# Which arm of a guard's branch stands next to it: `preferred_fallthrough_block=False` on a branch that is never taken into its body

## The chip, the cores, the metric

One core of one Trainium2 chip. The metric is the device time of one execution, in microseconds (us). Nine runs of the kernel before on one chip took 1291.71 to 1295.97 us, a spread of 4.3 us or 0.33%, so an effect of 2 us is at the edge of what times alone can show. This document therefore leans on traces, and on one length in them, called the **tail**: from the start of the last weight load on PE (TensorE) to the end of the span. The work ahead of that point is identical in the kernels compared, except where said, and in this tail PE has only 0.27 us of matmuls left to finish.

## The reference, cut to what matters

```python
x = A_x                                            # 2048 x 1024
h = _layernorm(x) * (1 + ca) + sa
x = x + ga * attention(h @ wq, k_cache, v_cache) @ wo   # 32 heads, softmax over 512 keys
h = _layernorm(x) * (1 + cb) + sb
x = x + gb * ((silu(h @ w_gate) * (h @ w_up)) @ w_down)
```

The kernel has a fast path that leaves out the maximum in the softmax. While it runs it bounds the scores. If the bound is over a limit, a flag is set, and a general path computes everything again. For the given inputs the flag is 0, so the general path never runs. It is still in the program: 16,921 instructions on PE, 3,010 on DVE (VectorE), 1,988 on ACT (ScalarE), 493 on SP (SyncE) and 59 on POOL (GpSimd).

## The kernel before

The guard, whole:

```python
def tile_adaLN_cond__sliding_block_cached__swiglu_ffn__prompt_kernel(tc, *args):
    nc = tc.nc
    with tc.tile_pool(name="guard", bufs=1) as gp:
        flag = gp.tile([1, 1], I32, name="flag")
        fast_path(tc, flag, *args)
        over = nc.values_load(flag[0:1, 0:1], min_val=0, max_val=1)   # L1243
        with tc.If(over > 0):                                         # L1244
            general_path(tc, *args)
```

The end of the fast path: the down projection of each tile of rows, whose outputs ACT sends off. The last tile is cut in three pieces.

```python
    def emit_down(cc, dh, t, widths=(512,)):
        ...
        for w in widths:
            ...                                   # 28 matmuls into d_ps          L1188
            nc.vector.tensor_tensor(out=r, in0=d_ps, in1=gb_bc[:, dsl], op=ALU.mult)          # L1192
            nc.vector.tensor_tensor(out=o, in0=r, in1=xt[cc * QT + t][:, dsl], op=ALU.add)    # L1194
            nc.scalar.dma_start(out=out2d[row:row + P, dsl], in_=o)                           # L1195
```

All weights are loaded by SP, whose last issue comes some 26 us before the last weight load on PE.

How the guard is built decides this case. The trace of before shows on each of the five engines one load of the flag (`TENSOR_LOAD`, L1243, 479 to 546 ns) and one compare-and-branch (L1244), at its own time: 686.7 us on POOL, 1258.4 on SP, 1284.3 on PE, 1285.9 on DVE, 1286.5 on ACT. Behind the branch stand three blocks:

- the **true block**, which is the general path;
- the **false block**, a few waits and semaphore updates, still of line 1244: on SP eight waits for all DMAs of the fast path, the last outputs among them; on ACT, DVE and PE one each, for their own last instruction;
- the **end block** of line 1271: on SP twelve closing waits for every engine and every DMA queue, then a barrier of all engines. Each engine has `DRAIN` instructions of this line; its first one (in before at 1288.3 us on PE, 1288.9 on DVE, 1289.2 on ACT and on SP) is read here as its arrival at the barrier.

The waits and updates are of semaphores, with which the program orders its engines and DMAs; the views list them as `EVENT_SEMAPHORE`. In the views a name with q at its end (SPq, ACTq) is an engine's instruction sequencer; PE's stands under PEldq.

Before the change the order is true, false, end. With the flag at 0 every engine jumps over its whole general path.

Of the kernel before, what the change touches and what calls it, by code (L numbers as in the profile page):

```python
# [1237 lines left out]
# [3 lines that stand above are left out]
        flag = gp.tile([1, 1], I32, name="flag")  # L1241
        fast_path(tc, flag, *args)
        over = nc.values_load(flag[0:1, 0:1], min_val=0, max_val=1)  # L1243
        with tc.If(over > 0):  # L1244
            general_path(tc, *args)


# [28 lines left out]
```

## Time and profile before

| | |
|---|---|
| median of 3 runs | 1292.92 us (1292.06 to 1293.39) |
| span of the profiled run | 1290.07 us, granted clock 0.999 |
| PE busy | 1271.4 us, 99% |
| start of the last weight load | 1284.63 us |
| tail | 5.44 us |

From the page of before, the span, the busiest engine, and the chain of waits that ended last:

```profile
span 1290.1 us, 15319 instructions
PE 1271.4 (99%) x6073; PEld 577.4 (45%) x6193; DVE 653.1 (51%) x1159; ACT 433.7 (34%) x625; POOL 1.2 (0%) x7
...
PE 95%; SPq 2%; DMA 1%; DVE 1%; issue 1%; DVEq 0%
```

PE bounds the kernel to its last matmul. The change touches no tile instruction, so only the tail can answer to it. Branches and semaphore instructions are not counted as busy; they show when the trace is asked for one source line. The view of line 1244 of before (count, then shortest/median/longest duration in ns, then the start of the first and of the last):

```profile
L1244 SPq EVENT_SEMAPHORE  x8: 17/17/17, 1265.3 to 1287.8; - x8
L1244 POOLq EVENT_SEMAPHORE  x5: 17/43/43, 687.1 to 687.5; - x5
L1244 POOLq COMPARE_BRANCH  x1: 45/45/45, 686.7 to 686.7; - x1
...
L1244 SPq COMPARE_BRANCH  x1: 58/58/58, 1258.4 to 1258.4; - x1
L1244 PEldq COMPARE_BRANCH  x1: 3762/3762/3762, 1284.3 to 1284.3; - x1
L1244 DVEq COMPARE_BRANCH  x1: 76/76/76, 1285.9 to 1285.9; - x1
L1244 ACTq COMPARE_BRANCH  x1: 65/65/65, 1286.5 to 1286.5; - x1
L1244 PEldq EVENT_SEMAPHORE  x1: 51/51/51, 1288.2 to 1288.2; - x1
L1244 DVEq EVENT_SEMAPHORE  x1: 21/21/21, 1288.8 to 1288.8; - x1
L1244 ACTq EVENT_SEMAPHORE  x1: 17/17/17, 1289.1 to 1289.1; - x1
```

Read each engine's branch against its next instruction. ACT branches at 1286.5 and goes on at 1289.1; DVE at 1285.9 and 1288.8; PE's branch itself lasts 3.8 us. POOL, with 59 instructions to jump over, goes on after 0.4 us. In each of the three gaps lies a DMA packet of one of the two instruction queues (from the trace's packet records, us from the last weight load):

```
before: PE   branch -0.29   packet of 16384 bytes  1.12 to 2.06   goes on at 3.53
        DVE  branch  1.27   packet of  8192 bytes  2.30 to 2.75   goes on at 4.15
        ACT  branch  1.90   packet of  8192 bytes  2.84 to 3.25   goes on at 4.50
```

(The first packet is of queue q8, whose 50 packets make 0.82 MB; the other two are of q14, and so are those put down to SP. Which packet is whose is inferred from the order and the times.) So the silence, 2.6 us on ACT, 2.9 on DVE and 3.8 on PE, is read as a wait for instructions that have to be fetched. Of before alone this is an inference; runs 7 to 9 and 11 test it.

SP is different. It branched at 1258.4, then spent 29 us waiting for output DMAs anyway, so its fetch cost nothing. The packet is there, at 1262.48 to 1262.79; before_again has one at the same place (4.0 and 4.6 us after SP's branch), and the traces in which SP falls through have none in the 25 us after the branch. The view of line 1271 of before, and then SP's waits after 1283 us:

```profile
L1271 SPq EVENT_SEMAPHORE  x14: 17/28/362, 1287.9 to 1290.0; - x14
...
L1271 SPq DRAIN  x3: 7/7/12, 1289.2 to 1289.5; - x3
L1271 PEldq DRAIN  x2: 8/8/8, 1288.3 to 1289.6; - x2
L1271 DVEq DRAIN  x2: 10/14/17, 1288.9 to 1289.5; - x2
L1271 ACTq DRAIN  x2: 8/8/8, 1289.2 to 1289.5; - x2
```

```profile
SPq L1271 <- DVEq L1244: 0.4, 1, 0.4
SPq L1271 <- ACTq L1244: 0.3, 1, 0.3
```

SP passes the last output's semaphore at 1287.8 (last wait of line 1244) and starts its closing waits at once, at 1287.9. Two of them are held by the late DVE and ACT. Its drain comes at 1289.2, and the end 0.86 us after it.

### The profile page before, as it was taken

The page shows a single profiled execution, that of the slowest core. Times are in us where ns is not written, and L with a number is a line of the kernel's source. Part 1 is how long each engine was busy: PE and PEld are TensorE (multiplying, and loading weights), DVE is VectorE, ACT ScalarE, POOL GpSimd, SP SyncE. Part 2 cuts the span into 40 slices and gives each one's busy share as a digit, 9 for nine tenths or more (in the row PEclk, how much of TensorE's full clock was granted, in tenths as well). Part 3 has the DMA queues.
Part 4 walks back from the last instruction along what each step waited for, and adds up shares of the span by engine and source line. Part 5 has one row for each costly group of instructions (what it writes and reads, how often), then busy time and mean ns, then how long its engine had stood idle before and what let it go on. Part 6 is the DMA issues. An engine that isn't in the chain of part 4 may idle for free.

```text
span 1290.1 us, 15319 instructions
## 1 busy us (share of the span) xinstructions
PE 1271.4 (99%) x6073; PEld 577.4 (45%) x6193; DVE 653.1 (51%) x1159; ACT 433.7 (34%) x625; POOL 1.2 (0%) x7
## 2 busy tenths in 40 slices
PE   8999999999999999999999999999999999999998
PEld 4444444444444444444444444444444444444444
DVE  5575668976688867597865641222122111222122
ACT  4755545554555555555552111011100111011100
POOL 0000000000000000000000000000000000000000
PEclk9999999999999999999999999999999999999999
DMA  9788565567365655455657485454536445454402
GB/s 290 242 277 256 178 196 139 170 174 219 103 193 144 189 146 175 146 165 143 185 194 238 127 240 182 136 192 131 171 105 220 157 148 178 135 192 131 147 18 84
DMA packets 219939, 221.08 MB, mean 171 GB/s; under 512 B 45385, under 2 KB 205129, under 8 KB 219858
## 3 DMA queue, kind: packets, MB, share of 16 engines
q1 hardware_dynamic: 214690, 215.54, 54.5%
q10 hardware_dynamic: 5168, 4.46, 1.0%
q8 instruction: 50, 0.82, 0.3%
q14 instruction: 31, 0.25, 0.1%
HBM read 207.63 MB, written 4.47 MB: 164 GB/s over the span
## 4 chain that ended last, share of the span: by engine, by line
PE 95%; SPq 2%; DMA 1%; DVE 1%; issue 1%; DVEq 0%
PE gu_ps L1168 29%; PE a_ps L1095 17%; PE q_ps L1018 17%; PE d_ps L1188 15%; PE o_ps L1079 9%; PE s_ps L1031 8%; SPq L664 1%; PE l_ps L1048 1%; SPq L703 1%; DMA hT<-xn 0%; DMA wq<-in_A_wq_dram 0%; DMA wu<-in_B_w_up_dram 0%; PE row_ps L777 0%; DVE guT L1174 0%; DVE xn L833 0%
## 5 line engine op out<-in xcount | busy, mean ns | idle before, releaser
L1033 ACT ACTIVATE pT<-s_ps 128x1024 bf16<-128x1024 f32 x256 | 252.0, 1026 | 72.8 <-PE s_ps L1031 67.3
L1095 PE MATMUL a_ps<-wo,oT 128*128 128x512 bf16 x972 | 238.9, 379 | 2.6
L1018 PE MATMUL q_ps<-hT,wq 128*128 128x512 bf16 x994 | 236.1, 379 | 0.8 <-DVE modT L753 0.3
L1173 ACT ACTIVATE sg<-gu_ps 128x512 bf16<-128x512 f32 x112 | 66.9, 597 | 486.0 <-PE gu_ps L1168 420.4
L1174 DVE TENSOR_TENSOR guT<-gu_ps,sg 128x512 bf16<-128x512 f32 x112 | 77.4, 691 | 280.0 <-ACT sg L1173 280.0
L1168 PE MATMUL gu_ps<-hT,wu 128*128 128x512 bf16 x878 | 210.1, 379 | 2.6 <-DMA wu<-in_B_w_up_dram 1.7
L1168 PE MATMUL gu_ps<-hT,wg 128*128 128x512 bf16 x877 | 210.0, 379 | 1.1
L1188 PE MATMUL d_ps<-wd,guT 128*128 128x512 bf16 (+2 forms) x934 | 193.2, 366 | 0.9
L1095 PEld LDWEIGHTS <-oT 128*128 128x128 bf16 x1024 | 100.0, 98 | 121.4 <-issue 1.3
L1018 PEld LDWEIGHTS <-wq 128*128 128x128 bf16 x1000 | 97.8, 98 | 118.5 <-DMA wq<-in_A_wq_dram 0.7
L1188 PEld LDWEIGHTS <-guT 128*128 128x128 bf16 x952 | 90.9, 98 | 103.0
L1168 PEld LDWEIGHTS <-wu 128*128 128x128 bf16 x896 | 87.6, 98 | 107.8 <-DMA wu<-in_B_w_up_dram 2.2
L1168 PEld LDWEIGHTS <-wg 128*128 128x128 bf16 x896 | 87.7, 98 | 105.7
L1038 DVE TENSOR_TENSOR psA<-pT 128x1024 bf16<-128x1024 bf16 x128 | 87.8, 686 | 89.0 <-ACT pT L1033 88.9
L1031 PE MATMUL s_ps<-qT,kT 128*128 128x512 bf16 x508 | 131.1, 379 | 0.7 <-ACT pT L1033 0.6
L1079 PE MATMUL o_ps<-pT,v_sb 128*128 128x512 bf16 x510 | 131.5, 380 | 0.2
L1081 ACT CAST oT<-o_ps 128x512 bf16<-128x512 f32 x128 | 74.5, 582 | 166.4 <-PE o_ps L1079 166.4
L914 DVE CAST qT<-q_ps 128x512 bf16<-128x512 f32 x128 | 87.5, 685 | 78.6 <-PE q_ps L1018 77.9
L1031 PEld LDWEIGHTS <-kT 128*128 128x128 bf16 x512 | 50.1, 98 | 61.5 <-issue 1.5
L1069 DVE TENSOR_TENSOR oT<-oT,rb 128x1024 bf16<-128x1024 bf16 x64 | 75.4, 1218 | 1.5 <-DMA rb<-r_d 1.5
L1079 PEld LDWEIGHTS <-v_sb 128*128 128x128 bf16 x512 | 47.4, 98 | 60.3 <-issue 7.7
L1040 DVE TENSOR_TENSOR psB<-psA 128x512 bf16<-128x512 bf16 x128 | 53.4, 417 | 0.6
(279 smaller groups left out, 443.2 us busy)
## 6 DMA issues: line engine op xcount, KB each, us to landing
wq<-in_A_wq_dram SPq DMA_DIRECT2D x64, 512.0 KB
rb<-r_d SPq DMA_DIRECT2D x64, 512.0 KB
wo<-in_A_wo_dram SPq DMA_DIRECT2D x64, 512.0 KB
wg<-in_B_w_gate_dram SPq DMA_DIRECT2D x56, 512.0 KB
wu<-in_B_w_up_dram SPq DMA_DIRECT2D x56, 512.0 KB
wd<-in_B_w_down_dram SPq DMA_DIRECT2D x56, 512.0 KB
wmr<-in_w_mod_dram SPq DMA_DIRECT2D x8, 1024.0 KB
out_dram<-o_sb ACTq DMA_DIRECT2D x31, 128.0 KB
```

The costliest lines, as they stand in the source:

```text
L914: nc.vector.tensor_copy(out=t, in_=q_ps)
L1018: nc.tensor.matmul(q_ps, lhsT=wq_tiles[(cc, h // 4, dt // 4)][:, dt % 4, (h % 4) * P:(h % 4 + 1) * P], rhs=hT[("h1", cc)][:, dt, :], start ...
L1031: nc.tensor.matmul(s_ps[:, i, :], lhsT=kT[:, kv, j * P:(j + 1) * P], rhs=qT[g], start=True, stop=True)
L1033: nc.scalar.activation(out=p[:, 2 * jj:2 * jj + 2, :], in_=s_ps, func=ACT.Exp, scale=scale)
L1038: nc.vector.tensor_tensor(out=a, in0=p[:, 0:2, :], in1=p[:, 2:4, :], op=ALU.add)
L1069: pin(nc.vector.tensor_tensor(out=oo, in0=oo, in1=rb, op=ALU.mult))
L1079: nc.tensor.matmul(o_ps, lhsT=v_sb[:, kv, j, :], rhs=pT[g][:, j, :], start=(j == 0), stop=(j == WT - 1))
L1081: nc.scalar.copy(out=oT[(cc, hg)][:, hi, :], in_=o_ps)
L1095: nc.tensor.matmul(a_ps, lhsT=oT[(cc, 2 * q + i)][:, hh % 4, t * P:(t + 1) * P], rhs=wo_tiles[(cc, q, dh, i)][:, hh % 4, :], start=(hh == ...
L1168: nc.tensor.matmul(ps[:, n, :], lhsT=gu_w[(cc, fg, nm, dt // 4)][:, dt % 4, fi * P:(fi + 1) * P], rhs=hT[("h2", cc)][:, dt, :], start=(dt ...
L1174: nc.vector.tensor_tensor(out=guT[(cc, fg)][:, fi, :], in0=ps[:, 1, :], in1=g, op=ALU.mult)
L1188: nc.tensor.matmul(d_ps, lhsT=guT[(cc, f // 4)][:, f % 4, t * P:(t + 1) * P], rhs=wd_tiles[(cc, dh, f // 4)][:, f % 4, c0:c0 + w], start=( ...
```

## The change

The intent: the usual case should fall through the branch and not jump.

```diff
-        with tc.If(over > 0):
+        with tc.If(over > 0, preferred_fallthrough_block=False):
             general_path(tc, *args)
```

The order of the built instructions tells more than the diff. Here PE's; the other engines are alike:

```
  L1243 TensorLoad flag
  L1244 CompareAndBranch
+ L1244 UnconditionalBranch
  L263  Ldweights ...                 (the general path begins)
  ...
  L578  Matmult ...                   (the general path ends)
- L1244 UnconditionalBranch x2
+ L1244 UnconditionalBranch
```

The order is now false, true, end. The usual case falls through into the false block, and that block ends with an unconditional jump over the general path to the end block.

A sentence is cut from the prediction that follows: it gave a rule for such waits that came from no trace of this case. No term of the sum goes with it: the sum came to +2.0 to +2.3 us, and its 2.6 to 2.9 us for SP are an estimate from the gaps of ACT (2.60) and DVE (2.88) in the trace of before.

> **What bounds the kernel.** The page of before: PE busy 1271.4 of 1290.1 us (99%), full clock; the chain that ended last is 95% PE. The change touches no tile instruction. It can move only the tail after the last matmul (1284.9 us), 5.2 us without PE work.
>
> **The tail now, from the trace's records of lines 1243, 1244 and 1271** (start times, us):
> - The last DVE op ends at 1285.56; ACT issues the last output DMA at 1285.59; it lands at 1287.76.
> - The branch is taken in the usual case, over the general path to the "false" block and end block behind it. After their compare-and-branch the engines go silent: ACT 1286.53 to 1289.12 (2.60 us), DVE 1285.90 to 1288.78 (2.88), PE 1284.34 to 1288.10 (3.76). In each gap lies an instruction-queue packet (8 KB; PE 16 KB) 0.9 to 1.4 us after the branch. POOL, whose general path is short, resumes after 0.42 us with none. [...]
> - SP branched at 1258.45; its fetch was hidden behind its wait for output DMAs. It passes the last output's semaphore at 1287.78, then makes 12 closing waits about 0.062 us apart, two of them held 0.5 us in all by DVE's and ACT's late arrival. Its drain at 1289.21 is followed 0.86 us later by the end.
>
> **What the change does.** By the instruction order, the false block now stands right after the branch, and ends in an unconditional jump over the general path to the end block. The far jump is not removed but moved: from before the false block's waits to after them.
> - ACT, DVE, PE: completion semaphores go out without the fetch (ACT 1286.6 instead of 1289.12); then they fetch, and reach the end barrier at about the old time. SP's 0.5 us of holds go.
> - SP: its false block waits for the last output (1287.76), and only then jumps over 493 instructions. Its fetch, hidden before, is exposed. Estimate from ACT's and DVE's gaps: 2.6 to 2.9 us.
>
> **Sum (estimate).** SP leaves its false block at 1287.86, resumes at 1290.5 to 1290.8, 12 waits 0.75 us, then 0.86 us: end 1292.1 to 1292.4 against 1290.07: +2.0 to +2.3 us, all on the critical path, 0.17%. Predicted 1295.0 us, range 1292.8 to 1296.6, mostly run scatter (1292.06 to 1293.39 before). Slower, though the wording promises a gain; within 2% almost surely.
>
> **What would show each step.**
> - ACT and DVE: line 1244's wait within about 0.1 us of the branch (PE: after its last matmul), then a gap of at least 2.5 us before line 1271.
> - SP: last wait of line 1244 at the output's landing, first of line 1271 2.5 to 3 us later, an 8 KB instruction packet between; then 12 waits 0.062 us apart, none held.
> - Nothing changed before 1284.9 us.
>
> **What would make it wrong.** If the sequencer fetches an unconditional jump's target while SP waits, or holds it already, the stall vanishes: about -0.5 us (1292.4). If SP's end block straddles a fetch boundary, it stalls twice: +4 us; by packet times I read a boundary every 128 instructions, none inside that block. Drift between sessions may hide 2 us.
>
> Chances: faster by over 2% 0.005, within 2% 0.985, slower 0.01.

## The result, and the profile after

| | before | after |
|---|---|---|
| runs | 1292.06 to 1293.42, median 1293.16 (4) | 1294.76 to 1297.00, median 1296.47 (4) |
| ratio, 95% interval | | 1.0025 (1.0011 to 1.0040) |
| span of the profiled run | 1290.07 | 1295.14 |
| start of the last weight load | 1284.63 | 1287.42 |
| tail | 5.44 | 7.72 |

All runs count as fast: the slowest of before is 0.11% above the fastest, the slowest of after 0.17%. A ratio is the mean time of one kernel's fast runs over that of the other's of the same rounds, so it is not quite the ratio of the medians quoted. The change is slower, by about 0.25%, well inside the 2% that count as the same. Of the 5.07 us between the two spans, 2.28 are in the tail, and 2.79 are ahead of it, where nothing was changed.

The page of after, the lines that answer to those above:

```profile
span 1295.1 us, 15444 instructions
PE 1280.3 (99%) x6193; PEld 577.9 (45%) x6193; DVE 653.1 (50%) x1159; ACT 433.7 (33%) x625; POOL 1.2 (0%) x7
...
PE 97%; DMA 1%; DVE 1%; SPq 0%; ACT 0%; issue 0%; DVEq 0%
```

(The 120 more matmuls are records that the first trace lacks, not work.) The tail, in the view of line 1244 of after:

```profile
L1244 SPq EVENT_SEMAPHORE  x8: 17/17/17, 1267.9 to 1290.9; - x8
...
L1244 SPq COMPARE_BRANCH  x2: 38/48/57, 1261.2 to 1291.0; - x2
L1244 PEldq COMPARE_BRANCH  x2: 95/1684/3273, 1287.1 to 1287.9; - x2
L1244 DVEq COMPARE_BRANCH  x2: 51/55/59, 1288.7 to 1288.9; - x2
L1244 ACTq COMPARE_BRANCH  x2: 38/44/51, 1289.3 to 1289.5; - x2
...
L1244 PEldq EVENT_SEMAPHORE  x1: 51/51/51, 1287.7 to 1287.7; - x1
L1244 DVEq EVENT_SEMAPHORE  x1: 21/21/21, 1288.8 to 1288.8; - x1
L1244 ACTq EVENT_SEMAPHORE  x1: 17/17/17, 1289.4 to 1289.4; - x1
```

Each engine now shows two branches: the compare, not taken, and the jump. ACT's and DVE's semaphores follow the compare within 0.1 us; the wait for instructions is gone from that place. It has moved behind the second branch, as the view of line 1271 of after shows:

```profile
L1271 SPq EVENT_SEMAPHORE  x14: 17/28/28, 1293.5 to 1295.1; - x14
...
L1271 SPq DRAIN  x3: 7/7/13, 1294.3 to 1294.6; - x3
L1271 PEldq DRAIN  x2: 8/40/73, 1291.2 to 1294.7; - x2
L1271 DVEq DRAIN  x2: 10/34/57, 1291.8 to 1294.6; - x2
L1271 ACTq DRAIN  x2: 8/44/80, 1292.1 to 1294.6; - x2
```

ACT jumps at 1289.5 and reaches its drain at 1292.1; counted from the last weight load that is 4.67, against 4.58 before. Nothing is won there. SP jumps at 1291.0, right after the last output's semaphore (1290.9), and its first closing wait starts at 1293.5. In the gap of 2.5 us lie four packets of the instruction queues. The first, of 8 KB, from 1291.91 to 1292.39, comes 0.92 us after SP's jump, as DVE's and ACT's came 0.94 to 1.02 us after their branches before; the other three come 0.6 us after DVE and ACT and 1.3 us after PE have gone on. That the first is SP's is inferred here; in run 8, where SP alone jumps far, a single packet lies in its gap. The fetch that was hidden before is now on the path that ends the kernel. The waits of 0.4 and 0.3 us on DVE and ACT are gone: the longest of SP's closing waits fell from 362 ns to 28.

Where the other 2.79 us come from: the view by windows of before and of after (length, then PE busy; the column after POOL is the granted PE clock):

```profile
10.00:24.00 14.00, 11.77 (x175) 8.09 (x175) 5.14 (x23) 4.79 (x9) 0.00 (x0) 0.88 1.18 302
760.00:770.00 10.00, 8.25 (x38) 3.57 (x38) 4.65 (x11) 1.20 (x2) 0.00 (x0) 1.00 0.62 203
```

```profile
10.00:24.00 14.00, 12.21 (x173) 8.15 (x174) 4.45 (x20) 4.29 (x8) 0.00 (x0) 0.76 1.23 296
760.00:770.00 10.00, 7.99 (x30) 3.09 (x29) 3.96 (x10) 1.01 (x2) 0.00 (x0) 0.83 0.69 214
```

The clock records say half speed for 3.4 us in the first window before, for 6.8 us after, and for another 3.4 us at 763.6 in the trace of after only. Weight load by weight load, after lags behind before by 0.84 us from 45 us on and by 2.79 us from 770 us on, and by a constant in between. Just ahead of 763.6 stands PE's wait for the DMA of a weight tile, 0.26 us longer in after, which is a part of the 1.95 us that are lost there; timeline of before, then of after:

```profile
762.27 1.04 PE L1168 MATMUL gu_ps<-hT,wu 128*128 128x512 bf16 x4 [1.75 <-DMA wu<-in_B_w_up_dram]
```

```profile
763.38 1.67 PE L1168 MATMUL gu_ps<-hT,wu 128*128 128x512 bf16 x4 [2.01 <-DMA wu<-in_B_w_up_dram]
```

Whether the new layout provokes this or it was chance is the first question for the experiments.

### The profile page after: what moved, and what is told of

Read it like the earlier page. It is cut to its first block, busy times and chain, and to the rows that moved or that the text cites. A ratio compares the mean times of both kernels' runs of the same rounds, so it can differ in the third digit from the quotient of the medians.

```text
span 1295.1 us, 15444 instructions
## 1 busy us (share of the span) xinstructions
PE 1280.3 (99%) x6193; PEld 577.9 (45%) x6193; DVE 653.1 (50%) x1159; ACT 433.7 (33%) x625; POOL 1.2 (0%) x7
## 3 DMA queue, kind: packets, MB, share of 16 engines
q10 hardware_dynamic: 5168, 4.46, 1.0%
## 4 chain that ended last, share of the span: by engine, by line
PE 97%; DMA 1%; DVE 1%; SPq 0%; ACT 0%; issue 0%; DVEq 0%
PE gu_ps L1168 29%; PE a_ps L1095 17%; PE q_ps L1018 17%; PE d_ps L1188 15%; PE o_ps L1079 9%; PE s_ps L1031 8%; PE l_ps L1048 1%; DMA wm<-in_w_mod_dram 1%; PE q_ps L938 0%; DMA hT<-xn 0%; DMA wu<-in_B_w_up_dram 0%; PE row_ps L777 0%; PE mod_ps L751 0%; SPq L664 0%; ACT pT L1033 0%; PE h_ps L925 0%
## 5 line engine op out<-in xcount | busy, mean ns | idle before, releaser
L1095 PE MATMUL a_ps<-wo,oT 128*128 128x512 bf16 x1024 | 241.9, 379 | 0.0
L1168 PE MATMUL gu_ps<-hT,wg 128*128 128x512 bf16 x896 | 212.8, 380 | 0.0
L1192 DVE TENSOR_TENSOR f<-d_ps,gb_bc 128x512 f32<-128x512 f32 (+2 forms) x34 | 22.5, 660 | 147.0 <-PE d_ps L1188 147.0
```

What stands on the lines that cost most here:

```text
L1095: nc.tensor.matmul(a_ps, lhsT=oT[(cc, 2 * q + i)][:, hh % 4, t * P:(t + 1) * P], rhs=wo_tiles[(cc, q, dh, i)][:, hh % 4, :], start=(hh == ...
L1168: nc.tensor.matmul(ps[:, n, :], lhsT=gu_w[(cc, fg, nm, dt // 4)][:, dt % 4, fi * P:(fi + 1) * P], rhs=hT[("h2", cc)][:, dt, :], start=(dt ...
```

## The experiments

Theory: the far jump is not removed but moved behind the false block's waits. That exposes SP's fetch, and nothing else costs. Rivals: the clock (A), the order of the blocks or the additional jump as such (B), the moved fetches of PE, DVE and ACT (C), a fixed cost of a far jump and not the fetch of a block (D), and later (E), chance in the landing of the last output. All twelve kernels gave a correct result. Kernels 1, 2, 3 and 5 of the list below shared one chip and the rounds of before on it, kernels 4, 6, 9 and 10 a second, and 7, 8, 11 and 12 a third; times are only compared within a chip. Kernels 2, 4, 6, 9, 10 and 11 ran once each, so their state is unknown; of these only the traces are used. Each entry of the list has one trace, so a tail or a landing below is a single reading. Times in the tail are us from the start of the last weight load. "Landing" is the receipt of the last output's DMA.

### 1 and 2: both kernels again

No edit.

> The changed kernel, unaltered, to separate the tail from the clock. 'Tail' is the time from the start of the last weight load to the end of the span: 5.44 us before, 7.72 us after in the first traces (+2.28). The other 2.79 us of the first pair's difference lie ahead of it: 0.84 us near 13 us and 1.95 us near 764 us, where the granted clock was 0.5. Theory (exposed fetch of SP, the clock by chance): tail 7.6 to 7.9 again; any throttled stretch of this trace lies elsewhere or has another length; the spans of the timed runs scatter by 1 to 3 us with their clock, and the ratio to before is about 1.0018 where clocks are alike. Rival A (the layout itself provokes the longer throttling): stretches at half clock near 13 us and 764 us again, and clocks clearly below those of before in every round, ratio 1.0035 or more.

> The kernel before, unaltered, one look for a second trace of its tail and clock. Theory: tail 5.3 to 5.6 us; stretches at half clock may come in other places and lengths than in its first trace. Rival A: only the short stretch of 3.4 us near 14 us, as in its first trace.

| trace | half clock, start and length | last weight load at | landing | SP jumps | SP goes on | end (tail) |
|---|---|---|---|---|---|---|
| before | 13.7: 3.4 | 1284.63 | 3.13 | hidden | hidden | 5.44 |
| before_again | 13.4: 3.4; 23.7: 3.4 | 1286.39 | 2.80 | hidden | hidden | 5.55 |
| after | 12.7: 6.8; 763.6: 3.4 | 1287.42 | 3.42 | 3.57 | 6.08 | 7.72 |
| after_again | 13.7: 3.4 | 1284.56 | 3.94 | 4.09 | 6.64 | 8.28 |

Time of five runs of after: 1294.42 to 1295.85, median 1295.26, against 1291.71 to 1295.97, median 1292.74, of nine runs of before. The ratio is 1.0018 (1.0004 to 1.0031), as expected.

Rival A falls: the second trace of after reaches its last weight load 0.07 us ahead of the first of before, and the second of before has a stretch at half clock more than the second of after. Of all fourteen traces, nine of them with the layout of after, only the first of after has half clock between 30 us and the last weight load. The 2.79 us did not come back; they are taken as chance. The wait for that weight tile was 1.66 us in after_again, 1.75 in before_again and 1.61 to 1.97 in all traces but the first of after, and the clock stayed up; only the wait of 2.01 us was followed by half clock.

A part of the expectation failed: the tail of after_again is 8.28 and not 7.6 to 7.9. From the landing to the end it takes 4.34 us, as in after (4.30). What moved is the landing. Run 11 goes after that.

### 3 to 5: all jumps near, and SP alone far

The general path is replaced by a stub that only has to exist, since it is never entered. Three kernels: the layout of after with a short stub, the layout of before with the same, and the layout of after with a stub of 492 SP instructions, so that SP's end block starts at instruction 1262 as in after.

```diff
         with tc.If(over > 0, preferred_fallthrough_block=False):
-            general_path(tc, *args)
+            stub_path(tc, *args, n_sp=16)      # near_after; spfar_after: n_sp=489; near_before: plain If
```

> The changed layout, with the general path (not executed with these inputs) cut to a stub of some 20 SP and 1 to 3 other instructions, so that every engine's jump lands a few instructions on. Theory (what costs is the fetch of a far target): no gap of over 0.5 us after any branch, tail 4.8 to 5.1 us, so about 2.7 us shorter than the changed kernel and 0.5 shorter than before. Rival B (the extra jump instruction, or the order of the waits, costs the time, whatever its distance): tail stays near 7.7 us, or at least clearly above 5.4.

> The layout of before with the same stub (about 20 SP instructions) in place of the general path. Theory: with all targets near, the two layouts do not differ: tail 4.8 to 5.1 us, within 0.15 us of the stub kernel with the changed layout; so some 0.5 us below before, whose holds of SP by DVE's and ACT's fetches are gone. Rival B (the order of the blocks itself matters): tail 0.3 us or more from the other stub kernel.

> As the stub kernel with the changed layout, but the stub holds 492 SP instructions, so that SP's end block starts at the same instruction number as in the changed kernel and SP alone jumps far. Theory (SP's exposed fetch is the whole cost): one gap of about 2.5 us on SP between lines of the false block and the end block, tail 7.2 to 7.6 us (it makes 4 closing waits fewer than the changed kernel). Rival C (the late arrival of PE, DVE or ACT after their own moved fetches is what costs): tail about 5 us, as with all jumps near.

Measured tails: 4.07 (near_after), 4.00 (near_before), 5.02 (spfar_after). The two layouts do not differ once the targets are near. But all three numbers lie under the expected ranges, and the reason is a fault of the experiment. The stub did not touch the output, so the build moved the last output behind the branch: ACT issues it at 1.7 and not at 0.96, and SP has jumped (at 1.1) long before it lands (3.2 to 3.3). Most of SP's fetch was hidden again. SP's gap was there, 2.6 us from its jump to its next instruction at 3.70, but only 0.95 us of it showed. Times against before: 0.9993 (0.9978 to 1.0008) for near_after and 0.9998 (0.9982 to 1.0013) for spfar_after.

### 6: the same, with SP's end block across a boundary of fetched blocks

Against spfar_after:

```diff
-            stub_path(tc, *args, n_sp=489)
+            stub_path(tc, *args, n_sp=458)
```

> As the kernel where SP alone jumps far, with 31 SP instructions fewer in the stub (461): by the packet times of the first traces, fetched blocks of SP begin at instruction 83 to 88 and every 128 from there, so the end block (1231 to 1243) now straddles a boundary. Theory (fetch of 8 KB blocks, the next block asked for only about 0.55 us after the engine resumes): SP stops twice, the second time for about 1.5 us inside its closing waits; tail 8.3 to 9.2 us although the jump is shorter. Rival D (a fixed cost of a far jump, or a fetched window larger than 128 instructions): tail as with 492 instructions, 7.2 to 7.6 us.

The tail is 6.82: below the expected 8.3 to 9.2, by the same fault, but 1.80 us **longer** than with the longer jump of spfar_after. SP stops twice: it goes on at 3.64, makes three closing waits, stops for 1.84 us, and goes on at 5.67. A second packet of 8 KB starts at 4.19, 0.55 us after SP went on. Rival D falls: here the shorter jump cost 1.80 us more, and what it had more was a second stop with a second packet. That a block is 128 SP instructions is inferred from before: among the 8 KB packets ahead of the branch are six that start when SP's trace is at its instruction 85, 213, 343, 470, 596 and 724, that is 126 to 130 apart. Nine times 128 after 85 is 1237; the end block of run 6 starts at 1231 and stopped after its first three instructions.

### 7 and 8: the stub mended

Now the stub also writes the last output rows, so everything stands ahead of the branch as in after.

```diff
+        nc.sync.dma_start(out=out[out.shape[0] - 128:, :], in_=t)     # in the stub
```

For run 8 the stub has `n_sp=488`; SP's end block then starts at instruction 1262, as in after.

> The stub kernels so far had a fault: their last output was issued after the branch, because the stub did not touch the output. Here the stub writes the last output rows, so everything stands before the branch as in the changed kernel; all jumps near. Times in us from the start of the last weight load. Theory: last output lands at 2.4 to 2.5 (as without the guard, 2.41, since no far fetch collides with it), end 1.5 to 1.8 after the landing, tail 4.0 to 4.3. Rival B (order of waits and the extra jump cost, whatever the distance): landing to end near 4.3, as in the changed kernel.

> As the corrected stub kernel, with 489 SP instructions in the stub, so that SP alone jumps far, to instruction 1262 as in the changed kernel. Theory: landing 2.4 to 2.6, SP resumes 2.5 to 2.6 after its jump, tail 6.4 to 6.8: 2.3 to 2.5 more than with SP near. Rival C (PE, DVE and ACT make the cost): tail as with SP near.

SP in near2_after, from the views of its branch line and of its end line:

```profile
L1264 SPq EVENT_SEMAPHORE  x8: 17/17/17, 1264.6 to 1287.1; - x8
L1264 SPq COMPARE_BRANCH  x2: 37/47/57, 1258.4 to 1287.1; - x2
```

```profile
L1291 SPq EVENT_SEMAPHORE  x10: 17/28/28, 1287.3 to 1288.6; - x10
```

and in spfar2_after:

```profile
L1264 SPq EVENT_SEMAPHORE  x8: 17/17/17, 1266.1 to 1288.4; - x8
L1264 SPq COMPARE_BRANCH  x2: 38/48/57, 1259.7 to 1288.5; - x2
```

```profile
L1291 SPq EVENT_SEMAPHORE  x10: 17/28/28, 1291.2 to 1292.5; - x10
```

The jump is the last of the two branches. With SP near, its first closing wait follows 0.2 us later; with SP far, 2.8 us later. Landing 2.41 and 2.40; tails 4.07 and 6.66, both as expected. Two parts of the expectation were missed: SP went on 2.78 us after its jump and not 2.5 to 2.6, and the tail is 2.59 us longer and not 2.3 to 2.5. SP's far jump alone costs 2.59 us. PE, DVE and ACT jump near in both, so rival C is not needed for it; rival B falls with near2_after, which has the block order and the additional jump of after and takes 1.66 us from landing to end, not 4.3. Times: 0.9986 (0.9971 to 1.0001) and 1.0006 (0.9990 to 1.0023) of before.

### 9: the other way round, SP alone near

The layout of after with the whole general path, whose loads ACT issues instead of SP. SP's jump passes one instruction.

```diff
-                nc.sync.dma_start(out=wq_h, in_=wq_v[:, :, h * Dh:(h + 1) * Dh])
+                nc.scalar.dma_start(out=wq_h, in_=wq_v[:, :, h * Dh:(h + 1) * Dh])
 (and all other loads of general_path)
```

> The changed layout with the whole general path, its SP loads issued by ACT instead: SP's jump passes one instruction, while PE, DVE and ACT still jump far. Theory: SP's gap of 2.5 us is gone, PE, DVE and ACT still show gaps of 2.3 to 3.8 us between the false block and the end block, and the tail is 5.3 to 5.5 us, set by ACT's late drain. Rival C (their fetches make the cost): tail near 7.7 us.

SP's two lines in the trace of this kernel, of its branches and of its closing waits:

```profile
L1244 SPq COMPARE_BRANCH  x2: 38/48/57, 1259.4 to 1289.6; - x2
```

```profile
L1271 SPq EVENT_SEMAPHORE  x14: 17/28/28, 1289.8 to 1291.4; - x14
```

SP goes on 0.2 us after its jump (4.05, 4.23). ACT, DVE and PE still reach their drains at 4.86, 4.46 and 4.39. From landing to end it takes 1.97 us, against 4.30 and 4.34 in the two traces of after: the whole excess is gone. Rival C falls. The tail is 5.87 and not 5.3 to 5.5, once more because of the landing, at 3.89; ACT's drain, which was expected to set the end, holds nobody (SP's longest closing wait is 28 ns).

### 10: no guard

Against before:

```diff
-        over = nc.values_load(flag[0:1, 0:1], min_val=0, max_val=1)
-        with tc.If(over > 0):
-            general_path(tc, *args)
```

> The fast path alone: no flag read, no branch, no general path (right for these inputs, not for all). It gives what the guard costs in all. Estimate: the last output lands as before, SP makes some 8 closing waits of 0.062 us, end 0.86 us after its drain: tail 4.3 to 4.8 us, against 5.44 before and 7.72 after. No gap on any engine after its last instruction but waiting for the landing.

The tail is 3.30, below the estimate, since the output lands at 2.41 and not at 3.13 as I had assumed. So, by one trace each, the guard costs 2.14 us of tail before (5.44) and 4.42 after (7.72), of a kernel of 1293 us. This version is right only for inputs under the bound.

### 11: PE alone far

Landings came at 2.40 to 2.41 in every kernel without a far jump of PE whose output is issued at 0.96, and at 2.80 to 3.94 in all with one. The packets say a good part of why. In after the last nine packets of the output, all others having gone by 2.06, start only as PE's 16 KB fetch ends:

```
trace          PE fetch         first of the late packets   landing
before         1.12 to 2.06     2.04                        3.13
after          1.43 to 2.39     2.37                        3.42
after_again    1.43 to 2.91     2.90                        3.94
spnear_after   1.88 to 2.87     2.85                        3.89
before_again   0.77 to 1.77     none late                   2.80
```

The late packets are not all of it. From the end of the last output packet to its receipt it takes 0.67 to 0.77 us in every trace in which PE jumps far, and 0.34 in those without (near2_after, spfar2_after, noguard). These 0.33 to 0.43 us come whether packets are late or not; they make up nearly all of the late landing of before_again (2.80) and of the kernel of run 12 (2.83), and their cause stays open.

In the layout of after PE's fetch starts later, because PE first falls into its false block, waits there for its last matmul, and only then jumps (compare at 1287.1, semaphore at 1287.7, jump at 1287.9). To test it, PE alone is made to jump far (against near2_after):

```diff
-            stub_path(tc, *args)
+            stub_path(tc, *args, n_pe=2000)
```

> As the corrected stub kernel, with 4002 PE instructions in the stub, so that PE alone jumps far. Second theory, from the packets of the traces: PE's 16 KB fetch [...] starts later (1.4 to 1.9 instead of 0.8 to 1.1), so the last nine output packets wait for its end. Expected: fetch at 1.3 to 2.9, last output packets starting when it ends, landing at 2.7 to 3.9 instead of 2.4; tail 4.9 to 5.5, set by PE's own late drain at 3.8 to 4.4. Rival E (the late landings are chance): landing 2.4 to 2.5 as with all near.

(Cut from it is a clause on what the fetch and the output share, which no trace at hand shows.)

PE's branch line in the trace of this kernel:

```profile
L1264 PEldq COMPARE_BRANCH  x2: 95/1804/3513, 1286.2 to 1286.9; - x2
```

PE's jump holds it for 3.5 us; the fetch lies at 1.43 to 2.64, the late output packets start at 2.62, and the landing is at 3.67 instead of 2.41. The tail is 5.33. These are as expected, and rival E falls. One part was missed: the tail is not set by PE's own drain, which comes at 4.04, when SP is still making its closing waits, none of them held; it is set by the late landing. So in this run the fetch stood in the output's way: the late packets began as it ended, and the landing came 1.26 us later. The theory's "nothing else costs" therefore does not hold: in the layout of after PE's later fetch costs the landing 0.3 to 0.8 us (3.42 and 3.94 against 3.13).

### 12: a version meant to beat both

The layout of before, SP's target near as in run 9, and the outputs of the last two tiles issued by SP, so that ACT has its branch and its fetch behind it in time.

```diff
+        out_eng = nc.sync if cc == NTC - 1 and dh == DH - 1 and t >= QT - 2 else nc.scalar
-            nc.scalar.dma_start(out=out2d[row:row + P, dsl], in_=o)
+            out_eng.dma_start(out=out2d[row:row + P, dsl], in_=o)
 (and the loads of general_path issued by ACT, as in run 9)
```

> A version meant to beat both: the layout of before; the general path's loads issued by ACT, so that SP's target is near; the last tiles' outputs issued by SP, so that ACT branches early and fetches in the shadow. DVE and PE still fetch late. Theory: SP's closing waits are held only by DVE, at about 4.15 after the last weight load; tail 5.0 to 5.4, against 5.44 and 5.55 in the two traces of before: 0.1 to 0.4 us, which the clock's scatter of 1 to 3 us hides, ratio 0.999 to 1.0005.

SP's waits after 1285 us in this kernel, the holds in its closing waits:

```profile
SPq L1272 <- DVEq L1245: 0.6, 1, 0.6
```

ACT's wait is gone (it branches at 1276.0 and goes on at 1278.6), DVE's is left, and the tail is 5.20, as expected: 0.24 to 0.35 us less than before. Five runs: 1292.23 to 1292.76, ratio 0.9989 (0.9976 to 1.0003). That is the same as before; the interval does not tell 0.3 us from nothing, and a ratio of 0.9989 is more than this edit can explain.

## Why the prediction was right, point by point

- **The far jump is moved, not removed, and SP pays.** Right, and shown three ways: SP alone far costs 2.59 us (7 against 8), SP alone near takes all of the excess away (9), and the block boundary adds a second stop (6). Predicted gap 2.6 to 2.9 us; measured 2.51 and 2.55 in the two traces of after, a little under it, and 2.78 in spfar2_after.
- **ACT, DVE and PE gain nothing.** Right: their drains come at 4.67, 4.40 and 3.80 in after, against 4.58, 4.26 and 3.69. The holds of SP are gone as predicted.
- **The tail.** Predicted 2.0 to 2.3 us longer; measured 2.28 in the first pair of traces and 2.73 in the second. The term that was mis-sized is the landing, taken as unchanged at 3.13. It was 3.42 and 3.94 in after, and the later packets of that output started only when PE's fetch, itself moved later by the change, had ended (11). The prediction has PE only as an engine that reaches the barrier at about the old time. That the first 2.28 lies in the predicted range is partly luck: the landing came 0.29 us later than assumed, and SP's gap was 0.1 to 0.4 us shorter.
- **"Nothing changed before 1284.9 us."** Wrong of the first pair: 2.79 us came from half clock and a wait 0.26 us longer, which did not come back in the second pair.
- **The time.** Predicted 1295.0 in 1292.8 to 1296.6; measured 1296.47, near the upper edge, and 1295.26 in the second session. From the medians the differences are 3.31 and 2.52 us (1296.47 - 1293.16 and 1295.26 - 1292.74), against 2.1 predicted. The tails alone make 2.28 and 2.73; in the profiled run of the first session the clock adds its share, and how much it adds to the others is not shown. That 1296.47 still lies in the range owes something to the range, which was made for run scatter: its upper edge is 0.13 us away.
- **Boundaries.** Read from packet times as every 128 SP instructions, none in the end block; run 6, where one was put there, agrees: SP stopped a second time, for 1.84 us. The "+4 us" for that case was an estimate; measured is a tail 1.80 us longer than in run 5, where SP stopped once.

What stays open: why, with a far jump of PE, the last receipt takes some 0.35 us more even when no packet is late (before_again), and why a wait of PE of 2.01 us was followed by half clock while waits of 1.61 to 1.97 us in thirteen other traces were not.

## What to carry to other kernels

Look at where a branch's usual target lies in each engine's instruction stream, not at which arm is called the fall-through. Here a far jump held SP, DVE and ACT for 2.5 to 3.0 us and PE for 3.3 to 3.9, in both layouts: the usual case still had to jump over a long block, so the fetch only moved. It should lie where the engine is waiting anyway. SP, done with its work 26 us ahead, had a jump that cost nothing in before; put behind its last wait, it cost 2.59 us (7 against 8). For differences of 0.2%, compare a stretch of the trace that ends the kernel, and check the clock in the rest, before explaining the times.
